# A conformer block's forward and backward pass on one core: b1 placed beside f1, another weight-gradient sum in b6, and the dK/dV partials added by TensorE instead of VectorE

## The chip, the cores and the metric

The kernel runs on one core of one Trainium2 chip. The metric is the time of one execution on the device, in microseconds (us). The names of the engines in the profile are PE (TensorE matmul), PEld (TensorE weight load), DVE (VectorE), ACT (ScalarE), POOL (GpSimd) and SP (SyncE, which issues most DMAs here).

## The reference, cut to what matters

The reference computes a branchformer block and all its gradients, for B = 2, T = 4000, D = 512, in bf16.

```python
def _fwd_reference(x, w_qkv, w_att_out, w_mlp_in, dw_csgu, w_mlp_out, dw_merge, w_merge):
    xa = _layernorm(x)
    q, k, v = split(xa @ w_qkv)
    p = softmax(q @ k.T * D ** -0.5)
    glob = (p @ v) @ w_att_out
    u, g = split(gelu(xa @ w_mlp_in))
    gc = depthwise_conv31(_layernorm(g), dw_csgu)
    loc = (u * gc) @ w_mlp_out
    m = concat(glob, loc)
    m = m + depthwise_conv31(m, dw_merge)
    return x + m @ w_merge

def reference(..., grad_out):
    out, vjp = jax.vjp(_fwd_reference, ...)
    return (out, *vjp(grad_out))      # 9 outputs
```

## The kernel before

The kernel is a sequence of stages, each a Python generator. Some run alone; some run as a main stage with a side stage that `interleave` feeds in between. A scheduler then orders the instructions of each engine at compile time, so an instruction may be placed ahead of its place in the program when its inputs are expected earlier. The order on the chip is fixed.

| stage | what it does |
|---|---|
| f1 | layer norm of x, Q, K, V, the two halves of the MLP, layer norm of g |
| f2 with f3, f4 | softmax attention; beside it the first convolution and `w_mlp_out` |
| f5, f6 | second convolution; output and the gradient of `w_merge` |
| b1 | gradient of m: `grad_out @ w_merge.T`, stored transposed |
| b2 | backward of the second convolution |
| b6 | gradient of the attention output, and of `w_att_out` |
| b7 with b3, b4, b5, weight gradients | attention backward; beside it everything of the local branch |
| b8 | gradients of x and `w_qkv` |

b1 depends on `grad_out` and `w_merge` only, and still stands alone after f6:

```python
    run_gen(gen_f1(k, x, w_qkv, w_mlp_in))
    ...
    run_gen(gen_f6(k, x, w_merge, grad_out, out_0, out_8))
    run_gen(gen_b1(k, grad_out, w_merge))
    # b2 ...
    run_gen(gen_b6(k, w_att_out, out_3))
```

b6 sums its weight gradient over all rows in four PSUM banks that it holds throughout (cut):

```python
        ps = ...tile_pool(name="b6_ps", bufs=2, space=PSUM)
        pst = ...tile_pool(name="b6_pst", bufs=2, space=PSUM)
        acc = psa.tile([128, 4, 512], F32, name="acc")
        ...
                    for dc in range(4):
                        nc.tensor.matmul(acc[:, dc, :], lhsT=attn[...], rhs=dgl[:sz, :], start=(it == 0), stop=(it == ntot - 1))
```

b7 splits the queries of a batch into four parts of eight tiles. For each part it walks over the 32 key tiles; for each key tile it sums dK and dV over the part's queries in two PSUM banks. Between parts the sums are kept in DRAM (`dkvp_d`) in bf16, and from the second part on (`hi > 0`, three quarters of the key tiles, 192 of 256) the stored partial is added on VectorE (cut):

```python
    ps_acc = ...tile_pool(name="b7_psacc", bufs=1, space=PSUM)     # dVacc, dKacc: one bank each
    ps_p   = ...tile_pool(name="b7_psp", bufs=2, space=PSUM)       # pp
    ...
                        for ii, qi in enumerate(half):
                            for c in range(4):
                                nc.tensor.matmul(pp, lhsT=dATh[...], rhs=VTb[...], ...)
                            nc.vector.scalar_tensor_tensor(out=dS, in0=pp, scalar=delta, in1=Eh, ...)   # (pp - delta) * Eh
                            nc.tensor.matmul(dVacc, lhsT=Eh[...], rhs=dAh[...], start=(ii == 0), stop=(ii == nh - 1))
                            nc.tensor.matmul(dKacc, lhsT=dS, rhs=Qh[...], start=(ii == 0), stop=(ii == nh - 1))
                            nc.tensor.transpose(out=pt, in_=dS, identity=k.ident)
                            evac(dSTg[...], pt)                                  # ScalarE
                        ...
                        else:      # hi > 0
                            nc.sync.dma_start(out=part[:ksz, :, :], in_=dst_part)
                            nc.vector.tensor_tensor(out=sumt[:ksz, 0, :], in0=dKacc[:ksz, :], in1=part[:ksz, 0, :], op=ALU.add)
                            nc.vector.tensor_tensor(out=sumt[:ksz, 1, :], in0=dVacc[:ksz, :], in1=part[:ksz, 1, :], op=ALU.add)
                            fin = wk.tile([128, 2, D], BF16, name="fin")
                            nc.scalar.copy(out=fin[:ksz, 0, :], in_=sumt[:ksz, 0, :])       # scaled in the last part
                            nc.scalar.copy(out=fin[:ksz, 1, :], in_=sumt[:ksz, 1, :])
                            nc.sync.dma_start(out=(dst_fin if last else dst_part), in_=fin[:ksz, :, :])
```

## Time and profile before

7046.74 us, median of 4 runs (7039.87 to 7050.35); the profiled run spans 7032.9 us.

The head of the page of the kernel before: span, busy time of each engine, and for 40 equal slices the busy share of TensorE and its granted clock, in tenths.

```profile
span 7032.9 us, 117349 instructions
PE 6004.2 (85%) x46132; PEld 3342.9 (48%) x46132; DVE 4098.4 (58%) x9164; ACT 2932.2 (42%) x6454; POOL 678.1 (10%) x502
PE   6775899799988788787888888899888899999999
PEclk8887999999999999999999999999999999999999
```

TensorE is the busiest engine, but not evenly: the first four slices (0 to 703 us), which hold f1 and its lead-out, are the emptiest and have the lowest clock.

The same kernel, busy times by stretches that I cut at the first and last matmuls of the stages: f1 with its lead-out, f2, f5 and f6, b1 and b2, b6, b7, b8. The columns are the stretch, its length, busy us of PE, PEld, DVE, ACT and POOL with instruction counts, granted clock, DMA share, GB/s.

```profile
0.00:657.80 657.80, 408.82 (x2572) 220.20 (x2573) 358.42 (x1249) 265.44 (x473) 7.22 (x22) 0.82 0.58 190
657.80:2062.30 1404.50, 1285.04 (x8123) 633.33 (x8123) 633.80 (x1715) 619.06 (x1379) 4.90 (x6) 0.97 0.41 101
2062.30:2655.50 593.20, 483.10 (x4806) 311.05 (x4805) 430.60 (x483) 238.91 (x283) 64.00 (x32) 0.95 0.49 166
2655.50:3080.50 425.00, 343.73 (x4050) 251.23 (x4049) 285.17 (x346) 259.21 (x344) 13.68 (x17) 0.95 0.46 161
3080.50:3268.90 188.40, 155.05 (x1048) 80.83 (x1045) 120.13 (x206) 85.51 (x144) 77.90 (x25) 0.95 0.78 249
3268.90:6502.40 3233.50, 2821.30 (x22658) 1601.89 (x22656) 1979.12 (x4489) 1361.02 (x3590) 436.51 (x336) 0.95 0.63 147
6502.40:7032.90 530.50, 507.14 (x2886) 244.42 (x2885) 291.12 (x678) 103.04 (x242) 73.87 (x64) 0.98 0.40 130
```

f1 has TensorE busy for 409 of 658 us; b7 for 2821 of 3233.5 us (87%).

Who TensorE waited for in f1 (30 to 600 us), then who waited for b7's VectorE sums; the columns are total us, times, longest:

```profile
PE pt L469 <- DVE gn L465: 132.2, 16, 8.8
PE pt L405 <- DVE xn L401: 37.6, 16, 30.0
...
PE dVacc L1163 <- DVE sumt L1189: 13.4, 2, 12.1
...
PE dKacc L1164 <- DVE sumt L1188: 1.5, 3, 0.8
```

In f1 TensorE waits for VectorE's two layer norms. The 30.0 us are the start of the kernel, before TensorE's first matmul. In b7 TensorE waited for the sums only 15 us in total.

The transposes of qkT and of gn in f1 of the kernel before (ns: shortest/median/longest), and, from the chain of waits at the end of b8, twelve dense matmuls of 512 columns (start, us, what):

```profile
L423 PE MATMUL pt<-ident,qkT x512: 216/219/230, 42.9 to 575.5; 128*128 128x128 bf16 x165, 128*32 128x128 bf16 x6
L469 PE MATMUL pt<-ident,gn x256: 182/314/314, 65.3 to 595.2; 128*128 128x128 bf16 x124, 32*128 32x32 bf16 x4
...
6970.30 2.62 PE pm L1255 x12
```

The median transpose takes 314 ns here, against 219 ns where TensorE runs densely. The Trainium skill ("TensorE: Matmul & The Clock Gate", Part 1) says why: TensorE's clock falls to half after an idle window of about 3.4 us. The trace agrees. The first transposes of gn come after 8.6 us of idle TensorE, and a few microseconds later TensorE runs densely; the two stretches, with the columns of the table above (the granted clock is the third number from the end):

```profile
65.30:67.30 2.00, 1.89 (x16) 1.62 (x16) 1.89 (x9) 1.04 (x2) 0.00 (x0) 0.50 0.04 14
77.00:80.00 3.00, 2.96 (x37) 2.22 (x36) 1.27 (x3) 2.83 (x6) 0.00 (x0) 1.00 0.47 154
```

At a granted clock of 0.50 the transposes of gn take 314 ns, at 1.00 those of qkT take 219 ns. A dense matmul of 512 columns takes 2.62 / 12 = 0.218 us; the same page, Part 2, gives 215.7 ns start to start at full clock, about 1% less.

Costs of the groups in b7 that the change touches, and of the one at its heart (dS), in the kernel before: busy us and mean ns of one, then the idle time before them and who ended it.

```profile
L1188 DVE TENSOR_TENSOR sumt<-dKacc,part 128x512 f32<-128x512 f32 x192 | 132.2, 688 | 74.1 <-PE dKacc L1164 55.6 <-DMA part<-dkvp_d 16.7 <-PE sA L648 0.5
L1189 DVE TENSOR_TENSOR sumt<-dVacc,part 128x512 f32<-128x512 f32 x192 | 132.1, 688 | 13.6 <-ACT fin L1194 3.8 <-ACT fin L1192 3.2 <-PE dVacc L1163 2.9
L1161 DVE SCALAR_TENSOR_TENSOR dS<-pp,delta_all,Eh 128x128 bf16<-128x128 f32 (+3 forms) x2048 | 654.8, 342 | 500.9 <-PE pp L1159 459.4 <-DMA Eh<-E_d 15.7 <-PE pt L1166 4.0
```

### The profile page before, as it was taken

The page shows a single profiled execution, that of the slowest core. Times are in us where ns is not written, and L with a number is a line of the kernel's source. Part 1 is how long each engine was busy: PE and PEld are TensorE (multiplying, and loading weights), DVE is VectorE, ACT ScalarE, POOL GpSimd, SP SyncE. Part 2 cuts the span into 40 slices and gives each one's busy share as a digit, 9 for nine tenths or more (in the row PEclk, how much of TensorE's full clock was granted, in tenths as well). Part 3 has the DMA queues.
Part 4 walks back from the last instruction along what each step waited for, and adds up shares of the span by engine and source line. Part 5 has one row for each costly group of instructions (what it writes and reads, how often), then busy time and mean ns, then how long its engine had stood idle before and what let it go on. Part 6 is the DMA issues. An engine that isn't in the chain of part 4 may idle for free. (4 is left out here: it accounts for less than half of the span.)

```text
span 7032.9 us, 117349 instructions
## 1 busy us (share of the span) xinstructions
PE 6004.2 (85%) x46132; PEld 3342.9 (48%) x46132; DVE 4098.4 (58%) x9164; ACT 2932.2 (42%) x6454; POOL 678.1 (10%) x502
## 2 busy tenths in 40 slices
PE   6775899799988788787888888899888899999999
PEld 3332444344446444654444455455444555554444
DVE  5663444344449663876777655444898454544555
ACT  3443444344447313764444434333555333333211
POOL 0000000000000110023444100000232000000111
PEclk8887999999999999999999999999999999999999
DMA  5555334535324655466444687877544868763533
GB/s 187 180 194 177 79 89 91 119 76 142 133 81 168 196 162 167 152 211 203 149 135 135 154 127 146 132 163 154 156 135 129 186 142 174 153 155 100 165 119 107
DMA packets 1253003, 1024.07 MB, mean 146 GB/s; under 512 B 486314, under 2 KB 1165057, under 8 KB 1244256
## 3 DMA queue, kind: packets, MB, share of 16 engines
q1 hardware_dynamic: 1214768, 979.15, 52.6%
q10 hardware_dynamic: 37680, 37.43, 1.6%
q8 instruction: 360, 5.90, 0.4%
q14 instruction: 195, 1.60, 0.1%
HBM read 609.16 MB, written 407.25 MB: 145 GB/s over the span
## 5 line engine op out<-in xcount | busy, mean ns | idle before, releaser
L80 ACT COPY dSTg<-pt 128x128 bf16<-128x128 bf16 (+3 forms) x2048 | 538.9, 263 | 1003.1 <-PE pt L1166 909.5
L1161 DVE SCALAR_TENSOR_TENSOR dS<-pp,delta_all,Eh 128x128 bf16<-128x128 f32 (+3 forms) x2048 | 654.8, 342 | 500.9 <-PE pp L1159 459.4
L1159 PE MATMUL pp<-VTb,dATh 128*128 128x128 bf16 (+1 forms) x8192 | 866.3, 222 | 9.0 <-DMA VTb<-VT_d 8.3
L1164 PE MATMUL dKacc<-Qh,dS 128*128 128x512 bf16 (+3 forms) x2048 | 747.5, 395 | 58.8 <-DVE dS L1161 46.0
L1159 PEld LDWEIGHTS <-dATh 128*128 128x128 bf16 (+1 forms) x8192 | 599.2, 100 | 295.2 <-issue 95.6
L1163 PE MATMUL dVacc<-dAh,Eh 128*128 128x512 bf16 (+3 forms) x2048 | 670.1, 387 | 23.8 <-DVE sumt L1189 13.4
L1201 PE MATMUL pq<-Kg,dSTg 128*128 128x512 bf16 (+3 forms) x2048 | 543.9, 384 | 43.1 <-DVE dQacc L1205 34.8
L517 PE MATMUL pm<-KT,QT 128*128 128x512 bf16 (+2 forms) x2048 | 518.1, 378 | 72.0 <-DMA KT<-KT_d 44.5
L548 PE MATMUL po<-V,ET 128*128 128x512 bf16 (+2 forms) x2048 | 507.8, 383 | 3.9 <-DVE ET L82 1.2
L1166 PE MATMUL pt<-ident,dS 128*128 128x128 bf16 (+3 forms) x2048 | 452.5, 221 | 32.9 <-ACT dSTg L80 27.3
L518 DVE TENSOR_SCALAR_CACHE_REDUCE S_sb<-pm 128x512 f32<-128x512 f32 (+2 forms) x512 | 344.2, 675 | 189.6 <-PE pm L517 185.2
L527 ACT ACTIVATE E<-S_sb,nb 128x512 bf16<-128x512 f32 (+2 forms) x512 | 356.9, 699 | 189.0 <-DVE nb L523 189.0
L1164 PEld LDWEIGHTS <-dS 128*128 128x128 bf16 (+3 forms) x2048 | 200.6, 99 | 314.6 <-DVE dS L1161 151.9
L1201 PEld LDWEIGHTS <-dSTg 128*128 128x128 bf16 (+3 forms) x2048 | 193.4, 98 | 262.7 <-issue 99.0
L517 PEld LDWEIGHTS <-QT 128*128 128x128 bf16 (+1 forms) x2048 | 188.8, 98 | 255.6 <-issue 81.3
L548 PEld LDWEIGHTS <-ET 128*128 128x128 bf16 (+2 forms) x2048 | 188.6, 98 | 222.7 <-issue 32.0
L617 POOL MEMSET Xw<- 128x896 bf16 x48 | 39.1, 847 | 2375.4 <-PE sA L648 833.4
L1205 DVE TENSOR_TENSOR dQacc<-dQacc,pq 128x512 f32<-128x512 f32 x192 | 131.3, 684 | 204.4 <-PE pq L1201 204.1
L1166 PEld LDWEIGHTS <-dS 128*128 128x128 bf16 (+3 forms) x2048 | 203.3, 99 | 80.9 <-issue 22.8
L1163 PEld LDWEIGHTS <-Eh 128*128 128x128 bf16 (+3 forms) x2048 | 183.0, 99 | 108.2 <-issue 45.6
L539 PE MATMUL pt<-ident,E 128*128 128x128 bf16 (+2 forms) x2048 | 195.4, 220 | 43.4 <-ACT E L527 40.4
L82 DVE COPY ET<-pt 128x1024 bf16<-128x1024 bf16 (+1 forms) x128 | 86.9, 679 | 236.8 <-PE pt L539 236.8
(278 smaller groups left out, 11117.2 us busy)
## 6 DMA issues: line engine op xcount, KB each, us to landing
E_d<-E SPq DMA_DIRECT2D x62, 1000.0 KB
part<-dkvp_d SPq DMA_DIRECT2D x186, 256.0 KB
Eh<-E_d SPq DMA_DIRECT2D x90, 512.0 KB
Kg<-K_d SPq DMA_DIRECT2D x248, 128.0 KB
dkvp_d<-fin SPq DMA_DIRECT2D x124, 256.0 KB
VTb<-VT_d SPq DMA_DIRECT2D x120, 256.0 KB
XT<-mT_d SPq DMA_DIRECT2D x16, 1536.0 KB
xn<-xn_d SPq DMA_DIRECT2D x42, 512.0 KB
```

The costliest lines, as they stand in the source:

```text
L80: self.nc.scalar.copy(out=out, in_=in_)
L517: nc.tensor.matmul(pm[:sq, :kw], lhsT=QT[:, c, :sq], rhs=KT[:, c, k0:k0 + kw], start=(c == 0), stop=(c == 3))
L518: nc.vector.tensor_scalar(out=S_sb[:sq, k0:k0 + kw], in0=pm[:sq, :kw], scalar1=1.0, scalar2=None, op0=ALU.mult, op1=ALU.max, accum_out=mx[ ...
L527: nc.scalar.activation(out=E[:sq, k0:k0 + kw], in_=S_sb[:sq, k0:k0 + kw], func=ACT.Exp, scale=scale, bias=nb[:sq], accum_out=ls[:sq, kb:kb ...
L539: nc.tensor.transpose(out=pt[:kwj, jj, :sq], in_=E[:sq, kj0:kj0 + kwj], identity=k.ident[:sq, :sq])
L548: nc.tensor.matmul(po[:sq, :], lhsT=ET[:kwj, j, :sq], rhs=V[:kwj, j, :], start=(j == 0), stop=(j == ntile - 1))
L1159: nc.tensor.matmul(pp[:sq, :ksz], lhsT=dATh[:, c, ii * 128:ii * 128 + sq], rhs=VTb[:, c, ks0:ks0 + ksz], start=(c == 0), stop=(c == 3))
L1161: nc.vector.scalar_tensor_tensor(out=dS[:sq, :ksz], in0=pp[:sq, :ksz], scalar=k.delta_all[:sq, col:col + 1], in1=Eh[:sq, ii, ks0:ks0 + ksz ...
L1163: nc.tensor.matmul(dVacc[:ksz, :], lhsT=Eh[:sq, ii, ks0:ks0 + ksz], rhs=dAh[:sq, ii, :], start=(ii == 0), stop=(ii == nh - 1))
L1164: nc.tensor.matmul(dKacc[:ksz, :], lhsT=dS[:sq, :ksz], rhs=Qh[:sq, ii, :], start=(ii == 0), stop=(ii == nh - 1))
L1166: nc.tensor.transpose(out=pt[:ksz, :sq], in_=dS[:sq, :ksz], identity=k.ident[:sq, :sq])
L1201: nc.tensor.matmul(pq[:sq, :], lhsT=dSTg[:ksz, slot, ii, :sq], rhs=Kg[:ksz, slot, :], start=(gi == 0), stop=(gi == len(gsubs) - 1))
```

## The change

The intent is to fill f1's TensorE gaps with b1, to give b6 more PSUM banks in rotation, and to take the two adds per key tile off VectorE: TensorE itself puts the stored partial into the bank, by a matmul with the identity, before the sums begin. The core of the diff (cut; unused new parameters left out):

```diff
-    run_gen(gen_f1(k, x, w_qkv, w_mlp_in))
+    with ExitStack() as region:
+        sps = region.enter_context(tc.tile_pool(name="sps_f1", bufs=1, space=PSUM))
+        main = gen_f1(k, region, x, w_qkv, w_mlp_in)
+        side = gen_b1(k, grad_out, w_merge, sps, ["sA"], sps, "sB", bufs=1, act_every=1)
+        interleave(main, side, B * len(k.tblocks) * 6, b1_units(k), finish_frac=0.9)
...
-    run_gen(gen_b1(k, grad_out, w_merge))
...
-        ps_mm = ctx.enter_context(tc.tile_pool(name="f1_psmm", bufs=4, space=PSUM))
+        ps_mm = ctx.enter_context(tc.tile_pool(name="f1_psmm", bufs=3, space=PSUM))
...  b6: evictions of the transposes all on ScalarE, and
-                        nc.tensor.matmul(acc[:, dc, :], ..., start=(it == 0), stop=(it == ntot - 1))
+                for dc in range(4):
+                    pw = ptile([128, 512], F32)          # 4 banks in rotation, with pm
+                    for j, (s0, sz) in enumerate(subs):
+                        nc.tensor.matmul(pw[:, :], ..., start=(j == 0), stop=(j == len(subs) - 1))
+                    wacc_add(k, first, wacc[:, dc, :], pw[:, :], dc)      # VectorE, into SBUF
...  b7:
+                        have_part = hi > 0
+                        if have_part:
+                            part = wk.tile([128, 2, D], BF16, name="part")
+                            nc.sync.dma_start(out=part[:ksz, :, :], in_=dst_part)
+                            nc.tensor.matmul(dKacc[:ksz, :], lhsT=k.ident[:ksz, :ksz], rhs=part[:ksz, 0, :], start=True, stop=False)
+                            nc.tensor.matmul(dVacc[:ksz, :], lhsT=k.ident[:ksz, :ksz], rhs=part[:ksz, 1, :], start=True, stop=False)
...
-                            nc.vector.tensor_tensor(out=sumt[:ksz, 0, :], in0=dKacc[:ksz, :], in1=part[:ksz, 0, :], op=ALU.add)
-                            nc.vector.tensor_tensor(out=sumt[:ksz, 1, :], in0=dVacc[:ksz, :], in1=part[:ksz, 1, :], op=ALU.add)
-                            ...two ScalarE casts of sumt...
+                            nc.scalar.copy(out=fin[:ksz, 0, :], in_=dKacc[:ksz, :])      # scaled in the last part
+                        nc.vector.tensor_copy(out=fin[:ksz, 1, :], in_=dVacc[:ksz, :])
```

In this text the third piece is called the fold, and its matmuls the seeds.

More of the change, by code (lines that the diff above doesn't have):

```diff
@@ L39, in chain, with delay @@
         yield from g
+def delay(n):
+    for _ in range(n):
+        yield
 def interleave(main, side, main_units, side_units, finish_frac=0.85):
@@ L309 @@
         run_gen(gen_conv(k, k.dm2T_d, k.dmcT_d, k.Zmb_d, C2, "b2", pst, "pt", psc, "po", bufs=2, onchip_out=True))
+    with ExitStack() as region:
+        psp = region.enter_context(tc.tile_pool(name="b6_ps", bufs=2, space=PSUM))
+        pst = region.enter_context(tc.tile_pool(name="b6_pst", bufs=3, space=PSUM))
+        run_gen(gen_b6(k, w_att_out, out_3, psp, ["pm", "pw"], pst, "pt", bufs=2))
     if STOP_AFTER == "b2":
         return debug_dump(k, [k.dmcT_d], keep=(0, 8))
-    run_gen(gen_b6(k, w_att_out, out_3))
     with ExitStack() as region:
@@ L371, in debug_dump, with gen_f1 @@
         zero_range(f0, si * per + cnt, (si + 1) * per if si < len(srcs) - 1 else n0)
-def gen_f1(k, x, w_qkv, w_mlp_in):
+def gen_f1(k, ctx, x, w_qkv, w_mlp_in):
     nc, tc, B, T, D = k.nc, k.tc, k.B, k.T, k.D
-    with ExitStack() as ctx:
+    if True:
         wp = ctx.enter_context(tc.tile_pool(name="f1_w", bufs=1))
@@ L596, in conv_units, with gen_conv @@
     return (C // 128) * per
-def gen_conv(k, src_d, dst_d, Z_d, C, tag, pst, tag_t, psc, tag_c, bufs=1, act_every=2, onchip_out=False):
+def gen_conv(k, src_d, dst_d, Z_d, C, tag, pst, tag_t, psc, tag_c, bufs=1, act_every=2, onchip_out=False, ctx_ext=None, xw_bufs=None, z_bufs=2):
     nc, tc, B, T = k.nc, k.tc, k.B, k.T
@@ L602, in gen_conv @@
     HC = 64
-    with ExitStack() as ctx:
+    with ExitStack() as ctx_own:
+        ctx = ctx_ext if ctx_ext is not None else ctx_own
         gtp = ctx.enter_context(tc.tile_pool(name=tag + "_gt", bufs=bufs))
-        xwp = ctx.enter_context(tc.tile_pool(name=tag + "_xw", bufs=bufs))
+        xwp = ctx.enter_context(tc.tile_pool(name=tag + "_xw", bufs=(xw_bufs or bufs)))
         wtp = ctx.enter_context(tc.tile_pool(name=tag + "_wt", bufs=bufs))
@@ L608, in gen_conv @@
         if onchip_out:
-            zp = ctx.enter_context(tc.tile_pool(name=tag + "_z", bufs=2))
+            zp = ctx.enter_context(tc.tile_pool(name=tag + "_z", bufs=z_bufs))
         evac = Evac(nc, act_every)
@@ L813, in gen_f6, with b1_units, gen_b1 @@
         yield
-def gen_b1(k, grad_out, w_merge):
+def b1_units(k):
+    return k.B * len(k.tblocks) * 3
+def gen_b1(k, grad_out, w_merge, psp, tags, pst_pool, tag_t, bufs=2, act_every=2):
     nc, tc, B, T, D = k.nc, k.tc, k.B, k.T, k.D
@@ L820, in gen_b1, with ptile @@
         wp = ctx.enter_context(tc.tile_pool(name="b1_w", bufs=1))
-        io = ctx.enter_context(tc.tile_pool(name="b1_io", bufs=2))
-        ps = ctx.enter_context(tc.tile_pool(name="b1_ps", bufs=4, space=PSUM))
-        pst = ctx.enter_context(tc.tile_pool(name="b1_pst", bufs=3, space=PSUM))
-        wmgT = load_wT(k, wp, pst, w_merge, "wmgT")
+        io = ctx.enter_context(tc.tile_pool(name="b1_io", bufs=bufs))
+        wmgT = load_wT(k, wp, pst_pool, w_merge, "wmgT", tag=tag_t)
         zero_pads(k, k.dm2T_d, C2)
-        evac = Evac(nc)
+        evac = Evac(nc, act_every)
+        ti = [0]
+        def ptile(shape, dt):
+            ti[0] += 1
+            return psp.tile(shape, dt, name=tags[ti[0] % len(tags)])
         for b in range(B):
@@ L833, in gen_b1 @@
                 for j, (s0, sz) in enumerate(subs):
-                    pt = pst.tile([128, 4, 128], BF16, name="pt")
+                    pt = pst_pool.tile([128, 4, 128], BF16, name=tag_t)
                     for c in range(4):
@@ L837, in gen_b1 @@
                     evac(doT[:, :, s0:s0 + sz], pt[:, :, :sz])
+                yield
                 dm2T = io.tile([128, 8, 512], BF16, name="dm2T")
                 for cc in range(8):
-                    pm = ps.tile([128, 512], F32, name="pm")
+                    pm = ptile([128, 512], F32)
                     for c in range(4):
@@ L843, in gen_b1, with wacc_add @@
                     evac(dm2T[:, cc, :w], pm[:, :w])
+                    if cc == 3:
+                        yield
                 store_dpart(k, nc.sync, k.dm2T_d[0:C2, b, :], 16 + t0, w, dm2T)
                 yield
-def wacc_add(k, first, acc_ap, ps_ap, i):
+def wacc_add(k, first, acc_ap, ps_ap, i, tmp_pool=None):
     nc = k.nc
     if first:
-        if i % 2:
+        if i % 2 or tmp_pool is not None:
             nc.scalar.copy(out=acc_ap, in_=ps_ap)
@@ L854, in wacc_add @@
             nc.vector.tensor_copy(out=acc_ap, in_=ps_ap)
+    elif tmp_pool is not None:
+        t = tmp_pool.tile([128, 512], F32, name="wacc_tmp")
+        nc.scalar.copy(out=t[:], in_=ps_ap)
+        nc.gpsimd.tensor_tensor(out=acc_ap, in0=acc_ap, in1=t[:], op=ALU.add)
     else:
@@ L1023, in gen_b5, with b6_units, gen_b6 @@
         yield
-def gen_b6(k, w_att_out, out_3):
+def b6_units(k):
+    return k.B * len(k.tblocks) * 2 + 1
+def gen_b6(k, w_att_out, out_3, psp, tags, pst_pool, tag_t, bufs=2):
     nc, tc, B, T, D = k.nc, k.tc, k.B, k.T, k.D
@@ L1029, in gen_b6, with ptile @@
         wp = ctx.enter_context(tc.tile_pool(name="b6_w", bufs=1))
-        io = ctx.enter_context(tc.tile_pool(name="b6_io", bufs=2))
+        io = ctx.enter_context(tc.tile_pool(name="b6_io", bufs=bufs))
         wk = ctx.enter_context(tc.tile_pool(name="b6_wk", bufs=2))
-        ps = ctx.enter_context(tc.tile_pool(name="b6_ps", bufs=2, space=PSUM))
-        pst = ctx.enter_context(tc.tile_pool(name="b6_pst", bufs=2, space=PSUM))
-        psa = ctx.enter_context(tc.tile_pool(name="b6_psa", bufs=1, space=PSUM))
-        waoT = load_wT(k, wp, pst, w_att_out, "waoT")
-        acc = psa.tile([128, 4, 512], F32, name="acc")
-        ntot = B * k.ntile
-        it = 0
-        evac = Evac(nc)
+        waoT = load_wT(k, wp, pst_pool, w_att_out, "waoT", tag=tag_t)
+        wacc = wp.tile([128, 4, D], F32, name="wacc_ao")
+        evac = Evac(nc, act_every=1)
+        ti = [0]
+        def ptile(shape, dt):
+            ti[0] += 1
+            return psp.tile(shape, dt, name=tags[ti[0] % len(tags)])
+        first = True
         for b in range(B):
@@ L1043, in gen_b6 @@
                 col0 = b * k.ntile + t0 // 128
-                dm2T = io.tile([128, 4, 512], BF16, name="dm2T")
-                load_dpart(k, nc.sync, dm2T, k.dm2T_d[0:D, b, :], 16 + t0, w)
+                dglT = io.tile([128, 4, 512], BF16, name="dglT")
+                load_dpart(k, nc.sync, dglT, k.dm2T_d[0:D, b, :], 16 + t0, w)
                 dmcT = io.tile([128, 4, 512], BF16, name="dmcT")
-                load_dpart(k, dma_eng(k), dmcT, k.dmcT_d[0:D, b, :], t0, w)
-                dglT = io.tile([128, 4, 512], BF16, name="dglT")
-                nc.gpsimd.tensor_tensor(out=dglT[:, :, :w], in0=dm2T[:, :, :w], in1=dmcT[:, :, :w], op=ALU.add)
+                load_dpart(k, nc.sync, dmcT, k.dmcT_d[0:D, b, :], t0, w)
+                nc.gpsimd.tensor_tensor(out=dglT[:, :, :w], in0=dglT[:, :, :w], in1=dmcT[:, :, :w], op=ALU.add)
                 attn = io.tile([128, 4, D], BF16, name="attn")
@@ L1053, in gen_b6 @@
                 datT = io.tile([128, 4, 512], BF16, name="datT")
+                dgl = io.tile([128, 4, D], BF16, name="dgl")
                 for j, (s0, sz) in enumerate(subs):
                     col = col0 + j
-                    pm = ps.tile([128, 512], F32, name="pm")
+                    pm = ptile([128, 512], F32)
                     for e in range(4):
@@ L1062, in gen_b6 @@
                                                    accum_out=k.delta_all[:sz, col:col + 1])
-                    pt = pst.tile([128, 4, 128], BF16, name="pt")
+                    pt = pst_pool.tile([128, 4, 128], BF16, name=tag_t)
                     for c in range(4):
@@ L1066, in gen_b6 @@
                     evac(datT[:, :, s0:s0 + sz], pt[:, :, :sz])
-                    pt2 = pst.tile([128, 4, 128], BF16, name="pt")
+                    pt2 = pst_pool.tile([128, 4, 128], BF16, name=tag_t)
                     for c in range(4):
                         nc.tensor.transpose(out=pt2[:sz, c, :], in_=dglT[:, c, s0:s0 + sz], identity=k.ident[:])
-                    dgl = wk.tile([128, D], BF16, name="dgl")
-                    evac(dgl[:sz, :], pt2[:sz].rearrange("p c e -> p (c e)"))
-                    for dc in range(4):
-                        nc.tensor.matmul(acc[:, dc, :], lhsT=attn[:sz, j, dc * 128:(dc + 1) * 128], rhs=dgl[:sz, :], start=(it == 0), stop=(it == ntot - 1))
-                    it += 1
+                    evac(dgl[:sz, j, :], pt2[:sz].rearrange("p c e -> p (c e)"))
                 store_tpart(k, nc.sync, k.dattn_d, b, t0, w, dat)
@@ L1077, in gen_b6 @@
                 yield
+                for dc in range(4):
+                    pw = ptile([128, 512], F32)
+                    for j, (s0, sz) in enumerate(subs):
+                        nc.tensor.matmul(pw[:, :], lhsT=attn[:sz, j, dc * 128:(dc + 1) * 128], rhs=dgl[:sz, j, :], start=(j == 0), stop=(j == len(subs) - 1))
+                    wacc_add(k, first, wacc[:, dc, :], pw[:, :], dc)
+                first = False
+                yield
         ot = wk.tile([128, 4, 512], BF16, name="ot3")
-        nc.vector.tensor_copy(out=ot[:], in_=acc[:])
+        nc.vector.tensor_copy(out=ot[:], in_=wacc[:])
         nc.sync.dma_start(out=out_3.rearrange("(c p) e -> p c e", p=128), in_=ot[:])
@@ L1108, in gen_b7 @@
     wk = ctx.enter_context(tc.tile_pool(name="b7_wk", bufs=2))
-    wk1 = ctx.enter_context(tc.tile_pool(name="b7_wk1", bufs=1))
     ps_acc = ctx.enter_context(tc.tile_pool(name="b7_psacc", bufs=1, space=PSUM))
@@ L1153, in gen_b7 @@
                         dKacc = ps_acc.tile([128, D], F32, name="dKacc")
+                        r0 = k0 + ks0
+                        dst_fin = k.dqkv_d[b, r0:r0 + ksz, D:3 * D].rearrange("p (a d) -> p a d", a=2)
+                        dst_part = k.dkvp_d[b, r0:r0 + ksz, :].rearrange("p (a d) -> p a d", a=2)
+                        have_part = hi > 0
[4 more added lines that the diff above has]
+                            nc.tensor.matmul(dVacc[:ksz, :], lhsT=k.ident[:ksz, :ksz], rhs=part[:ksz, 1, :], start=True, stop=False)
                         for ii, qi in enumerate(half):
@@ L1162, in gen_b7 @@
                                                            in1=Eh[:sq, ii, ks0:ks0 + ksz], op0=ALU.subtract, op1=ALU.mult)
-                            nc.tensor.matmul(dVacc[:ksz, :], lhsT=Eh[:sq, ii, ks0:ks0 + ksz], rhs=dAh[:sq, ii, :], start=(ii == 0), stop=(ii == nh - 1))
-                            nc.tensor.matmul(dKacc[:ksz, :], lhsT=dS[:sq, :ksz], rhs=Qh[:sq, ii, :], start=(ii == 0), stop=(ii == nh - 1))
+                            nc.tensor.matmul(dVacc[:ksz, :], lhsT=Eh[:sq, ii, ks0:ks0 + ksz], rhs=dAh[:sq, ii, :], start=(ii == 0 and not have_part), stop=(ii == nh - 1))
+                            nc.tensor.matmul(dKacc[:ksz, :], lhsT=dS[:sq, :ksz], rhs=Qh[:sq, ii, :], start=(ii == 0 and not have_part), stop=(ii == nh - 1))
                             pt = ps_t.tile([128, 128], BF16, name="pt")
@@ L1169, in gen_b7 @@
                                 yield
-                        r0 = k0 + ks0
-                        dst_fin = k.dqkv_d[b, r0:r0 + ksz, D:3 * D].rearrange("p (a d) -> p a d", a=2)
-                        dst_part = k.dkvp_d[b, r0:r0 + ksz, :].rearrange("p (a d) -> p a d", a=2)
-                        if nparts == 1:
-                            fin = wk.tile([128, 2, D], BF16, name="fin")
-                            nc.scalar.activation(out=fin[:ksz, 0, :], in_=dKacc[:ksz, :], func=ACT.Copy, scale=scale)
-                            nc.vector.tensor_copy(out=fin[:ksz, 1, :], in_=dVacc[:ksz, :])
-                            nc.sync.dma_start(out=dst_fin, in_=fin[:ksz, :, :])
-                        elif hi == 0:
-                            part = wk.tile([128, 2, D], BF16, name="part")
-                            nc.scalar.copy(out=part[:ksz, 0, :], in_=dKacc[:ksz, :])
-                            nc.vector.tensor_copy(out=part[:ksz, 1, :], in_=dVacc[:ksz, :])
-                            nc.sync.dma_start(out=dst_part, in_=part[:ksz, :, :])
-                        else:
-                            part = wk.tile([128, 2, D], BF16, name="part")
-                            nc.sync.dma_start(out=part[:ksz, :, :], in_=dst_part)
-                            last = (hi == nparts - 1)
-                            sumt = wk1.tile([128, 2, D], F32, name="sumt")
-                            nc.vector.tensor_tensor(out=sumt[:ksz, 0, :], in0=dKacc[:ksz, :], in1=part[:ksz, 0, :], op=ALU.add)
-                            nc.vector.tensor_tensor(out=sumt[:ksz, 1, :], in0=dVacc[:ksz, :], in1=part[:ksz, 1, :], op=ALU.add)
-                            fin = wk.tile([128, 2, D], BF16, name="fin")
-                            if last:
-                                nc.scalar.activation(out=fin[:ksz, 0, :], in_=sumt[:ksz, 0, :], func=ACT.Copy, scale=scale)
-                            else:
-                                nc.scalar.copy(out=fin[:ksz, 0, :], in_=sumt[:ksz, 0, :])
-                            nc.scalar.copy(out=fin[:ksz, 1, :], in_=sumt[:ksz, 1, :])
-                            nc.sync.dma_start(out=(dst_fin if last else dst_part), in_=fin[:ksz, :, :])
@@ new lines, in gen_b7 @@
+                        last = (hi == nparts - 1)
+                        fin = wk.tile([128, 2, D], BF16, name="fin")
+                        if last:
+                            nc.scalar.activation(out=fin[:ksz, 0, :], in_=dKacc[:ksz, :], func=ACT.Copy, scale=scale)
+                        else:
+                            nc.scalar.copy(out=fin[:ksz, 0, :], in_=dKacc[:ksz, :])
+                        nc.vector.tensor_copy(out=fin[:ksz, 1, :], in_=dVacc[:ksz, :])
+                        nc.sync.dma_start(out=(dst_fin if last else dst_part), in_=fin[:ksz, :, :])
```

## The prediction

> **What bounds the kernel now.** One core, 7032.9 us in the profile, TensorE busy 85% (page). I cut the span by first and last starts of each stage's matmuls and read the busy table by stretches: f1 0-600 us, f2 to f6 up to 2660, b1 2660-2820, b2 to 3080, b6 3080-3275, b7 with its side work 3275-6503, then b8. TensorE is 87% busy in b7 (2818 of 3228 us), 97% where no side work runs (6300-6503). In f1 it is busy only 408 of 570 us; the waits there name VectorE: 132 us for gn, 38 us for xn (layer norm chains). f1's granted clock is 0.84 and its transposes take 314 ns against 219 elsewhere. The Trainium skill ("TensorE: Matmul & The Clock Gate", Part 1) says TensorE falls to half clock after an idle window of about 3.4 us; f1's gn waits of up to 8.8 us agree.
>
> **What changes.**
> 1. b1 moves into f1's gaps. b1 needs 136 us of TensorE and alone takes about 160 us, with about 8 us at each seam. Now it has one PSUM buffer per tag, all evictions on ScalarE (512-wide ones 576 ns), and f1 keeps 3 matmul banks of 4. Load of the joint stage: ScalarE 263 + about 115 = 378 us, TensorE 408 + 136 = 544 us, DMA share about 0.68. At the 88% that TensorE reaches in other interleaved stages it takes about 618 us plus 30 us of start, against 600 + 160: saves about 110 us (60 to 145). One seam fewer: about 10 us more.
> 2. b6: same matmuls. VectorE loses 64 datT copies (413 ns, 26 us), gains 60 adds (683 ns, 41 us); ScalarE gains 37 us; more rotating banks. 195 us becomes about 187.
> 3. b7: for three quarters of the key tiles (192) two 688 ns VectorE adds and about 1.24 us of ScalarE casts become one 679 ns VectorE copy and one ScalarE copy of about 0.6 us: VectorE -134 us, ScalarE -125 us. TensorE gains 384 identity matmuls of 512 columns. Dense chains in b8 run at 0.22 us each (12 in 2.62 us), so +84 us on the engine that bounds b7. What is removed hardly stalled it: matmuls waited for sumt 15 us in total. sumt runs at 3943-5065 and from 5470, mostly where TensorE is 88 to 93% busy and VectorE about 50%; the VectorE-bound stretches (b3 to 3943, most of b5) have none. Some 25 us come back through shorter bank turnover and fewer eviction waits: net +58 us.
>
> **On the critical path:** -110 -10 -8 +58 = -70 us. Predicted 6977 us, 0.99 of before, range 6895 to 7055. Chances: faster by over 2% 0.12, within 2% 0.85, slower 0.03.
>
> **What would show it.** The b1 stretch between f6 and b2 is gone; first softmax matmul at 650 to 700 us (657.8 before); TensorE share in the joint stage 80% or more, clock above 0.84, gn waits well below 132 us. From b7's first matmul to its last pq the span grows by 30 to 85 us, TensorE busy there by about 80, VectorE falls by about 130; waits of the seed matmuls for part under 20 us. b6 180 to 195 us. b8 unchanged.
>
> **What would make it wrong.** If single-buffered b1 units stall TensorE on each ScalarE eviction (about 0.8 us, 9 per block, 16 blocks) the joint stage saves under 50 us. If seeds wait for the part load or for emptied banks at each key tile, b7 loses 150 us or more. If VectorE relief removes more of b7's 410 us of TensorE idle than I think, b7 stays level and the total is near 6920.

## The result, and the profile after

The changed kernel takes 6958.52 us, median of 8 runs (6949.26 to 6975.37), against 7045.73 us for the kernel before in the same rounds (12 runs). The ratio is 0.9878, 95% interval 0.9868 to 0.9888.

The changed kernel by stretches, cut at the same matmuls, with the same columns as before:

```profile
0.00:710.40 710.40, 528.56 (x3373) 273.75 (x3374) 362.76 (x1253) 365.56 (x669) 7.89 (x23) 0.90 0.67 217
710.40:2111.60 1401.20, 1285.54 (x8124) 635.11 (x8124) 634.62 (x1715) 618.97 (x1379) 4.90 (x6) 0.97 0.40 101
2111.60:2707.90 596.30, 485.11 (x4806) 311.74 (x4805) 430.68 (x483) 238.70 (x283) 64.02 (x32) 0.94 0.49 165
2707.90:2977.10 269.20, 207.67 (x3257) 180.11 (x3257) 226.29 (x247) 203.55 (x244) 13.00 (x16) 0.97 0.39 148
2977.10:3152.90 175.80, 153.96 (x1038) 76.52 (x1034) 124.14 (x201) 112.95 (x210) 79.19 (x25) 0.97 0.81 262
3152.90:6432.50 3279.60, 2891.54 (x23045) 1638.56 (x23044) 1885.34 (x4300) 1245.52 (x3398) 436.35 (x336) 0.96 0.63 145
6432.50:6962.70 530.20, 507.43 (x2886) 244.96 (x2885) 291.15 (x678) 103.03 (x242) 73.86 (x64) 0.98 0.40 130
```

Line by line against the table before, in us:

| stretch | before | after | difference |
|---|---|---|---|
| f1 (after: with b1) | 657.8 | 710.4 | +52.6 |
| f2, f5, f6 | 1997.7 | 1997.5 | -0.2 |
| b1 and b2 (after: b2 alone) | 425.0 | 269.2 | -155.8 |
| b6 | 188.4 | 175.8 | -12.6 |
| b7 and its side work | 3233.5 | 3279.6 | +46.1 |
| b8 | 530.5 | 530.2 | -0.3 |
| span | 7032.9 | 6962.7 | -70.2 |

So two pieces gave 116 us and b7 gave 46 us of it back.

TensorE's waits in the joint stage of the changed kernel (30 to 650 us), and the transposes of gn there:

```profile
PE sA L863 <- ACT dm2T L85: 28.5, 44, 1.0
PE pt L480 <- DVE gn L476: 25.1, 9, 8.6
...
PE pt L416 <- DVE xn L412: 5.8, 9, 1.5
...
L480 PE MATMUL pt<-ident,gn x256: 182/229/314, 73.6 to 647.8; 128*128 128x128 bf16 x124, 32*128 32x32 bf16 x4
```

The waits for the layer norms fell from 140 us (without the 30 us at the start) to 31 us, and b1's own work stands in their place. A new wait is small: b1's matmuls wait 28.5 us for ScalarE to empty their single bank. The median transpose fell from 314 to 229 ns and the granted clock of the stretch up to the first softmax matmul rose from 0.82 to 0.90. One gap is left as it was: just before that matmul TensorE is idle for 44 us in both kernels, waiting for the load of KT, and b1 was not placed there.

The groups of b7 in the changed kernel that replace those shown before:

```profile
L1196 PE MATMUL dKacc<-part,ident 128*128 128x512 bf16 x192 | 75.3, 392 | 2.9 <-DMA part<-dkvp_d 0.6 <-ACT fin L1219 0.4
L1197 PE MATMUL dVacc<-part,ident 128*128 128x512 bf16 x192 | 75.3, 392 | 21.8 <-DMA part<-dkvp_d 21.5 <-DVE fin L1220 0.2
L1220 DVE CAST fin<-dVacc 128x512 bf16<-128x512 f32 (+1 forms) x256 | 175.6, 686 | 36.0 <-DMA dkvp_d<-fin 12.2 <-PE sA L717 9.3 <-DMA dqkv_d<-fin 4.4
L1205 DVE SCALAR_TENSOR_TENSOR dS<-pp,delta_all,Eh 128x128 bf16<-128x128 f32 (+3 forms) x2048 | 679.0, 343 | 676.0 <-PE pp L1203 614.6 <-DMA Eh<-E_d 11.4 <-PE dKacc L1208 10.4
```

VectorE now waits for TensorE's pp 615 us before its dS, where it waited 459 us: it became idler. A caution on busy sums: all 2048 dS are in both traces, and 2048 x 342 ns would be 700 us, not 654.8. The busy time is the time that is covered, so instructions that overlap in the trace count once. The stretch table's VectorE difference in b7, -94 us, is the fall of the time in which VectorE is busy at all; the sum of durations fell by more, -264.3 for the sums and +132 for the 192 more dV copies, -132 us.

### The profile page after: what moved, and what is told of

The parts are those of the page before. It is cut to its first block, busy times and chain, and to the rows that moved or that the text cites. A ratio compares the mean times of both kernels' runs of the same rounds, so it can differ in the third digit from the quotient of the medians.

```text
span 6962.7 us, 117900 instructions
## 1 busy us (share of the span) xinstructions
PE 6059.8 (87%) x46516; PEld 3360.7 (48%) x46516; DVE 3955.0 (57%) x8874; ACT 2888.3 (41%) x6424; POOL 679.2 (10%) x502
## 5 line engine op out<-in xcount | busy, mean ns | idle before, releaser
L1205 DVE SCALAR_TENSOR_TENSOR dS<-pp,delta_all,Eh 128x128 bf16<-128x128 f32 (+3 forms) x2048 | 679.0, 343 | 676.0 <-PE pp L1203 614.6
L1203 PE MATMUL pp<-VTb,dATh 128*128 128x128 bf16 (+1 forms) x8192 | 923.6, 221 | 6.7 <-DMA VTb<-VT_d 6.1
L1208 PE MATMUL dKacc<-Qh,dS 128*128 128x512 bf16 (+3 forms) x2048 | 768.9, 393 | 51.3 <-DVE dS L1205 41.6
L1203 PEld LDWEIGHTS <-dATh 128*128 128x128 bf16 (+1 forms) x8192 | 622.2, 99 | 323.7 <-issue 91.9
L1207 PE MATMUL dVacc<-dAh,Eh 128*128 128x512 bf16 (+3 forms) x2048 | 729.1, 386 | 6.8 <-DVE fin L1220 3.4
L1298 POOL TENSOR_TENSOR gx<-t,dot 128x512 bf16<-128x512 f32 x64 | 73.9, 1154 | 1531.0 <-DMA dzT<-dzT_d 1115.6
```

The lines of the kernel that those rows point to most:

```text
L1203: nc.tensor.matmul(pp[:sq, :ksz], lhsT=dATh[:, c, ii * 128:ii * 128 + sq], rhs=VTb[:, c, ks0:ks0 + ksz], start=(c == 0), stop=(c == 3))
L1205: nc.vector.scalar_tensor_tensor(out=dS[:sq, :ksz], in0=pp[:sq, :ksz], scalar=k.delta_all[:sq, col:col + 1], in1=Eh[:sq, ii, ks0:ks0 + ksz ...
L1207: nc.tensor.matmul(dVacc[:ksz, :], lhsT=Eh[:sq, ii, ks0:ks0 + ksz], rhs=dAh[:sq, ii, :], start=(ii == 0 and not have_part), stop=(ii == nh ...
L1208: nc.tensor.matmul(dKacc[:ksz, :], lhsT=dS[:sq, :ksz], rhs=Qh[:sq, ii, :], start=(ii == 0 and not have_part), stop=(ii == nh - 1))
```

## The experiments

The theory, as in the prediction: b1 fills gaps, and the fold is paid by TensorE, which bounds b7, while the VectorE time that it frees was mostly not in the way. Rivals: the fold pays, and b7 is longer for another reason; or the fold's cost is a wait (for the part load, for emptied banks) and not work.

The kernels are built from the changed kernel, or from the kernel before where the label ends in "only". Twelve ran. Each had three or five timed rounds.

### The three pieces one by one

`all_but_fold` is the changed kernel with the b7 of before (the last block of the diff undone); `fold_only`, `b1_only` and `b6_only` are the kernel before with one piece of the diff alone.

> The changed kernel with the old b7 (partials added by VectorE). Theory (TensorE bounds b7, the fold is paid by it): the whole fold is a loss here, b7 goes back from 3280 us to about 3234 us, total about 6913 us, 0.981 of before, clearly faster than the changed kernel. Rival (the fold pays, and the 46 us longer b7 comes from another order of the side work or the new start of the stage): total 6955 us or more.

> The old kernel with the new b7 alone. Theory: b7 grows by 35 to 60 us, total about 7090 us, 1.006 of before; VectorE busy falls by about 100 us or more and buys less than the 70 to 84 us of TensorE work cost. Rival (longer b7 was a side effect of the other two parts): 7045 us or less.

> The old kernel with b1 moved into f1 alone. Theory: saves about 103 us (joint stage +53, stretch after f6 -156), total about 6943 us, 0.985 of before. Rival (part of that gain comes from b6 no longer needing all eight banks behind b2): saves under 90 us.

> The old kernel with the new b6 alone. Theory: 188 us become about 176 us by more rotating banks, total about 7034 us, 0.998 of before, just at the edge of what these rounds resolve. Rival (the b6 gain is due to what runs before it): no difference.

| kernel | median us | ratio to before | 95% interval |
|---|---|---|---|
| all_but_fold | 6913.6 | 0.9827 | 0.9814 to 0.9841 |
| fold_only | 7075.8 | 1.0054 | 1.0040 to 1.0068 |
| b1_only | 6932.5 | 0.9846 | 0.9833 to 0.9860 |
| b6_only | 7027.3 | 0.9982 | 0.9969 to 0.9995 |

Multiplied by 7040 us, b1 gives 108 us, b6 gives 13 us and the fold costs 38 us; the sum, -83 us, is what the changed kernel shows (0.9878, -86 us). Within the noise the pieces simply add up. The rival that the longer b7 came from its neighbours is out: the fold alone lengthens b7 from 3233.5 to 3276.4 us, and without it b7 is back. b7's stretch in `fold_only` and in `all_but_fold`:

```profile
3270.30:6546.70 3276.40, 2898.68 (x23041) 1637.84 (x23039) 1877.80 (x4297) 1246.40 (x3398) 436.40 (x336) 0.95 0.63 145
...
3143.00:6373.80 3230.80, 2819.00 (x22661) 1602.78 (x22660) 1985.58 (x4492) 1360.11 (x3590) 437.21 (x336) 0.95 0.63 147
```

TensorE is 80 us busier with the fold, VectorE 108 us less, ScalarE 114 us less, and the stage is longer by 46 us. `b6_only` shows the b6 stretch falling from 188.4 to 168.5 us in its profile, as much as or more than in the changed kernel, so that gain does not come from what runs before it.

### The fold's cost and its relief, each by itself

`zero_seeds_and_adds` is `all_but_fold` with seeds of zeros and the adds kept:

```diff
+    zseed = res.tile([128, D], BF16, name="zseed");  nc.vector.memset(zseed[:], 0.0)
...
+                        if hi > 0:
+                            nc.tensor.matmul(dKacc[:ksz, :], lhsT=k.ident[:ksz, :ksz], rhs=zseed[:ksz, :], start=True, stop=False)
+                            nc.tensor.matmul(dVacc[:ksz, :], lhsT=k.ident[:ksz, :ksz], rhs=zseed[:ksz, :], start=True, stop=False)
```

> The changed kernel with the old b7 and its VectorE adds, plus 384 identity matmuls of a block of zeros at the places of the seeds: the TensorE cost of the fold by itself, without its relief of VectorE and ScalarE and without waiting for part. Theory (TensorE work is the cost): 55 to 84 us longer than the 6914 us without it, so about 6970 to 6998 us, longer than the changed kernel. Rival (the cost of the fold is the wait for the part load and for the emptied banks at the start of each key tile): under 20 us longer, as zeros are always there.

`no_seeds_no_adds` is the changed kernel without the two seed matmuls (wrong dK and dV; the partials are still loaded and stored, but nothing uses what is loaded):

```diff
-                            nc.tensor.matmul(dKacc[:ksz, :], lhsT=k.ident[:ksz, :ksz], rhs=part[:ksz, 0, :], start=True, stop=False)
-                            nc.tensor.matmul(dVacc[:ksz, :], lhsT=k.ident[:ksz, :ksz], rhs=part[:ksz, 1, :], start=True, stop=False)
```

> The changed kernel with the seed matmuls taken out and nothing in their place; dK and dV are wrong on purpose (they hold the last part of the queries only). The relief by itself. Theory: about 25 to 40 us shorter than the 6914 us with adds (the relief that the prediction put at 25 us), 60 to 84 us shorter than the changed kernel. Rival (VectorE relief is worth nothing here): equal to 6914 us.

`fold_at_end` moves the same two matmuls behind the query loop, as the last of each accumulation (`start=False, stop=True`).

> The changed kernel with the two identity matmuls as the last of each accumulation instead of the first: same TensorE work, same relief, but part is needed some 8 us later. The trace of the changed kernel shows 43 us of weight-load waits for part, 21.5 us of them two stalls of 10.9 us. Theory (work, not waiting): within 20 us of the changed kernel's 6958 us. Rival (waiting for part is most of the cost): 30 us or more faster.

| kernel | adds | seeds | b7 in the profile | median us | ratio, 95% interval |
|---|---|---|---|---|---|
| no_seeds_no_adds | no | no | 3184.0 | 6862.2 | 0.9744 (0.9728 to 0.9759) |
| all_but_fold | VectorE | no | 3230.8 | 6913.6 | 0.9827 (0.9814 to 0.9841) |
| zero_seeds_and_adds | VectorE | zeros | 3270.3 | 6950.0 | 0.9869 (0.9853 to 0.9884) |
| fold_at_end | no | last | 3270.9 | 6951.9 | 0.9872 (0.9858 to 0.9886) |
| changed kernel | no | first | 3279.6 | 6958.5 | 0.9878 (0.9868 to 0.9888) |

b7's stretch in `no_seeds_no_adds`, then `zero_seeds_and_adds`, then `fold_at_end`:

```profile
3148.50:6332.50 3184.00, 2808.88 (x22662) 1595.99 (x22661) 1859.30 (x4300) 1243.37 (x3398) 436.87 (x336) 0.96 0.64 149
...
3150.40:6420.70 3270.30, 2899.20 (x23046) 1638.82 (x23045) 1983.64 (x4493) 1353.53 (x3590) 436.99 (x336) 0.95 0.63 145
...
3150.10:6421.00 3270.90, 2894.40 (x23045) 1634.29 (x23044) 1869.94 (x4300) 1255.82 (x3398) 436.92 (x336) 0.95 0.63 145
```

The first two missed the stated sizes. Zeros cost 40 us of b7 (36 us of the medians), under the 55 to 84 us of the theory and over the 20 us of the rival. Taking both away was worth 47 us of b7 against the adds (25 to 40 expected) and 96 us against the changed kernel (60 to 84 expected). What holds is the structure. With the seeds in, b7 takes 3270 us (3280 in the changed kernel) whether VectorE adds as well or not: against `fold_at_end`, 114 us of VectorE and 98 us of ScalarE work make 0.6 us of difference. Without the seeds, b7 with the adds is 47 us longer than the kernel that leaves them out. And the seeds cost 87 to 96 us on top of that kernel, 40 us on top of the one with adds. The cost of work on two engines here is not a sum. The corner with neither has a wrong result, though, and how much of its 47 us is relief from the adds comes below.

Whether it is work or waiting, `fold_at_end` was meant to tell, and does not: part is needed later there, but its trace still has TensorE waiting 21.0 us for it, in three stalls, where the changed kernel had 21.5 us in two. Its time is not distinguishable from the changed kernel's. The zeros tell it better: they are always there, so their seeds cannot wait for part, and they still lengthen b7 by 40 us. The traces also show that the stalls for part are not new. The two in the changed kernel come 797 and 1094 us after b7's first pp. In the kernel before, TensorE stalls at nearly the same places, 11.0 us at 792 us (for ScalarE's dSTg) and 12.1 us at 1076 us (for VectorE's sum, which was waiting for part).

The cleanest piece is the last part of b7, where no side work is left; its length is read between the last dQ evictions of parts seven and eight. It is 302.8 us without both, 310.6 with the adds and 317.3 in the changed kernel. The seeds' 64 matmuls there account for 14.5 us, which is 0.227 us each, close to the dense rate of 0.218 us. That closeness is not general: the same part takes 312.1 us in `fold_at_end`, so there the same 64 matmuls cost 9.3 us, 0.145 us each.

### Is it VectorE's time, or the emptying of the banks?

`direct_add` adds on VectorE from PSUM straight into the bf16 tile, without the float32 sum and its ScalarE casts. `gpsimd_add` evicts as the changed kernel does, into a float32 tile, and lets GpSimd add; `evict_then_vector_add` is the same with the last add on VectorE.

```diff
+   # direct_add (dK is kept scaled from the first part on)
+   nc.vector.scalar_tensor_tensor(out=fin[:ksz, 0, :], in0=dKacc[:ksz, :], scalar=scale, in1=part[:ksz, 0, :], op0=ALU.mult, op1=ALU.add)
+   nc.vector.tensor_tensor(out=fin[:ksz, 1, :], in0=dVacc[:ksz, :], in1=part[:ksz, 1, :], op=ALU.add)
...
+   # gpsimd_add; nc.vector in place of nc.gpsimd: evict_then_vector_add
+   nc.scalar.activation(out=sumt[:ksz, 0, :], in_=dKacc[:ksz, :], func=ACT.Copy, scale=scale)
+   nc.vector.tensor_copy(out=sumt[:ksz, 1, :], in_=dVacc[:ksz, :])
+   nc.gpsimd.tensor_tensor(out=fin[:ksz, :, :], in0=sumt[:ksz, :, :], in1=part[:ksz, :, :], op=ALU.add)
```

> The changed kernel with b7's partials added by VectorE straight from PSUM into the bf16 output tile (dK kept scaled from the first part on), so the float32 sum and its two ScalarE casts are gone and no TensorE work is added. Same VectorE time as before, ScalarE about 240 us less. Theory (TensorE bounds b7): 0 to 25 us below the 6914 us of the version without the fold, so 6890 to 6914 us and the fastest so far. Rival (VectorE time matters): no gain over 6914 us, or a loss if the scaled add takes longer than 0.69 us.

> The changed kernel with neither seeds nor VectorE adds: dK is evicted by ScalarE (scaled) and dV by VectorE into a float32 tile, as in the run without seeds and adds, and GpSimd, which is idle in these stretches, adds the stored partial. Right result. If the 51 us of relief measured there hold with the add done elsewhere: 6860 to 6885 us, 0.974 to 0.978 of before, over 2% faster and the fastest of all. Rival (GpSimd slows VectorE while both work in SBUF, or its add of about 2.3 us per key tile delays the stores): 6900 us or more.

> The same kernel as the one with the add on GpSimd, but the add from the float32 tile on VectorE. Banks are emptied as early (one copy on each of two engines, side by side), VectorE works more (about 0.68 us of copy and 1.4 to 2.8 us of add per key tile). Theory A (the relief is the earlier emptying of the two banks): b7 near 3184 us, total 6860 to 6890 us. Theory B (the relief is VectorE's time between two dS): b7 as long as with the adds from PSUM or longer, 3230 us or more, total 6910 us or more.

| kernel | b7 in the profile | median us | ratio, 95% interval |
|---|---|---|---|
| direct_add | 3222.5 | 6910.5 | 0.9813 (0.9799 to 0.9827) |
| gpsimd_add | 3223.5 | 6908.4 | 0.9812 (0.9799 to 0.9826) |
| evict_then_vector_add | 3253.0 | 6935.6 | 0.9852 (0.9839 to 0.9866) |

b7's stretch in `gpsimd_add`, then in `evict_then_vector_add`:

```profile
3154.20:6377.70 3223.50, 2825.76 (x22661) 1613.17 (x22660) 1881.84 (x4300) 1246.13 (x3398) 846.35 (x528) 0.95 0.64 148
...
3162.80:6415.80 3253.00, 2849.40 (x22662) 1602.86 (x22661) 2072.04 (x4492) 1250.33 (x3398) 439.13 (x336) 0.95 0.64 146
```

The add of the partial in `gpsimd_add`, then in `evict_then_vector_add`:

```profile
L1219 POOL TENSOR_TENSOR fin<-sumt,part 128x1024 bf16<-128x1024 f32 x192 | 408.3, 2128 | 1606.6 <-ACT sumt L1217 777.8 <-ACT dSTg L85 434.9 <-DVE dS L1196 175.2
...
L1219 DVE TENSOR_TENSOR fin<-sumt,part 128x1024 bf16<-128x1024 f32 x192 | 235.9, 1230 | 64.0 <-ACT sumt L1217 43.0 <-DMA part<-dkvp_d 20.7
```

`evict_then_vector_add` missed the number of its theory A: each bank is emptied by one copy, on two engines, as without the adds, and b7 takes 3253 us, not 3184. Its VectorE is busy 190 us more than in `gpsimd_add` (2072 against 1882) and b7 is 30 us longer. VectorE's time does have a price there, as theory B says. `direct_add` takes 207 us from ScalarE (1360 to 1153 us) and gains 8 us in b7; ScalarE is hardly the limit. Its 6910.5 us cannot be told from the 6913.6 us of `all_but_fold`, so this run does not decide between its theory and its rival.

`gpsimd_add` missed. On TensorE, VectorE and ScalarE it does the work of `no_seeds_no_adds`, yet b7 is 3223.5 us, not 3184. GpSimd did not slow VectorE: its adds took 2128 ns and the mean dS 342 ns, as in `all_but_fold`. So of the 47 us between `all_but_fold` and `no_seeds_no_adds`, only 7 us came back when the adds left VectorE with a right result, although VectorE was about as free (1882 against 1859 us busy) and the banks were emptied in the same way. The 47 us can therefore not be put down to these two alone. Where the other 40 us went is open. They are not spread evenly: cut at the last dQ evictions, the fourth of b7's eight parts takes 392.8 us in `gpsimd_add` and 388.8 in `all_but_fold`, but 367.8 in `no_seeds_no_adds`, which alone is 25 and 21 us. There TensorE is busy 348 us at a granted clock of 0.98, against 356 us at 0.96 in `gpsimd_add`. The two kernels differ in what depends on part, in what the stores wait for, and in the compile-time order of every engine; no run here separates these.

### The joint stage

`b1_evict_alternate` lets VectorE and ScalarE take turns at b1's evictions; `b1_two_banks` gives b1's matmuls two banks and f1's two instead of three.

```diff
-        side = gen_b1(k, grad_out, w_merge, sps, ["sA"], sps, "sB", bufs=1, act_every=1)
+        side = gen_b1(k, grad_out, w_merge, sps, ["sA"], sps, "sB", bufs=1, act_every=2)         # b1_evict_alternate
+        side = gen_b1(k, grad_out, w_merge, sps, ["sA", "sC"], sps, "sB", bufs=1, act_every=1)   # b1_two_banks
-        ps_mm = ctx.enter_context(tc.tile_pool(name="f1_psmm", bufs=3, space=PSUM))
+        ps_mm = ctx.enter_context(tc.tile_pool(name="f1_psmm", bufs=2, space=PSUM))              # b1_two_banks
```

> The changed kernel with b1's evictions alternating between VectorE and ScalarE instead of all on ScalarE. In the joint stage ScalarE is 59% busy, VectorE 57%, and TensorE waits 41 us for ScalarE's emptying of b1's single banks and 31 us for layer norm on VectorE. Theory (VectorE's layer norm chain is what must not be delayed): first softmax matmul the same or up to 15 us later. Rival (ScalarE's queue holds up b1's single banks): 10 to 25 us earlier.

> The changed kernel with two banks for b1's matmuls and two, not three, for f1's. Of the joint stage's waits 33 us are b1's matmuls waiting for their one bank. Theory (f1's 20 matmul groups per block need their banks more than b1's 8): within 10 us of the changed kernel or slower. Rival (the one bank of b1 is what keeps the joint stage at 710 us): 15 to 30 us faster.

Alternating costs: the first softmax matmul comes at 733.9 us, 23.5 us later than in the changed kernel (the theory had 0 to 15), and the total is 6983.7 us, ratio 0.9920 (0.9906 to 0.9933). TensorE's waits in its joint stage show how:

```profile
PE sA L863 <- DVE dm2T L87: 32.8, 27, 3.5
PE pt L480 <- DVE gn L476: 20.2, 6, 8.6
...
PE sA L863 <- ACT dm2T L85: 8.9, 14, 0.7
```

b1's single bank now waits for VectorE, 1.2 us at a time, which runs half of its evictions beside the layer norms; on ScalarE the same wait was 0.65 us at a time (28.5 us, 44 times). The waits for gn did not grow, so the theory's direction was right and its reason was not: the waits that grew are b1's for VectorE, not those for layer norm. Two banks for b1 (717.2 us, total 6969.4 us, ratio 0.9899, 0.9885 to 0.9912) do not help: b1's 28.5 us wait goes, and the wait for gn rises from 25.1 to 38.4 us, that for doT from 8.2 to 19.2.

### The fastest version

Leaving the fold out beats both kernels: 0.9827 for `all_but_fold`, 0.9813 and 0.9812 for the two other ways to add, whose intervals overlap with it. None of the three is shown to be over 2% faster than the kernel before, as each interval reaches past 0.98. Against the kernel before that is about 130 us (0.0188 x 7040), against the changed kernel 36 to 46 us (0.9878 less 0.9827 or 0.9812).

## Why the prediction was right or wrong

The time was right: 6977 us predicted, 6958.5 measured, inside the range, and "within 2%" was the class. The sum of its terms was -70 us; the profiles give -70.2 us, the timed rounds -86 us. That the first two agree to 0.2 us is luck: b1 saved 17 us less than forecast, the fold cost 12 us less and b6 gave 5 us more.

- **b1 (-110 and -10 predicted).** Right, at 12 to 17 us under the sum. The stretches give +52.6 - 155.8 = -103 us, the piece alone 108 us. The way was the foreseen one: waits for the layer norms fell from 140 to 31 us, the joint stage has TensorE busy for 526 us of the 620 between 30 and 650 us (85%), and the clock rose. The feared stall of b1's single banks was there but small, 28.5 us and not 9 x 16 x 0.8 = 115 us, as each wait lasted 0.65 us, and there were 44, not 144.
- **The window for the first softmax matmul (650 to 700 us)** did not follow from the prediction's own numbers: 648 us for the joint stage plus the 58 us that lay between f1's end and that matmul make 706. Measured: 710.4. That was a slip of writing, not of the sum.
- **b6 (-8 predicted, 180 to 195 us).** Right in sign; 175.8 us lies below the stated window. The piece alone gave 13 us.
- **The fold (+84, -25, net +58).** The net was close: +46 in the profile, 38 us (fold_only) in the timed rounds. The mechanism, that TensorE pays for what VectorE saves, is shown by the experiments: seeds of zeros lengthen b7. But the two terms were mis-sized, and nearly cancelled. Put the seeds in first, and they cost 40 us and not 84; take the adds out after that, and not 25 us come back but none (b7 grows by 0.6 to 9 us). Take the adds out first, and 47 us come back in the kernel with a wrong result, 7 us in `gpsimd_add`; the seeds then cost 96 us (87 at the end) or 56 us. The step that failed is "Some 25 us come back", and with it the adding of two fixed terms: what each is worth depends on whether the other is there. I took the 25 us from TensorE's direct waits for sumt (15 us) and a guess. That the net still came out near 58 us is in part luck.
- **Seeds' waits for part under 20 us.** Wrong by little: 21.5 us before the matmuls, in two stalls of 10.9 us at most. TensorE stalled about as long at the same places in the kernel before.
- **TensorE +80, VectorE -130 in b7.** +70 by busy time; -94 by busy time, -132 by the sum of durations.
- **b8 unchanged.** Right.

## What to carry to other kernels

Work that depends on the inputs alone belongs in the gaps of a stage whose busiest engine waits on another one's chain of small operations; here 136 us of TensorE work cost 53 us there, and its evictions did better on the engine that does not run that chain (23.5 us). Before moving an add from VectorE to TensorE, look at which engine bounds that very stretch: here 384 identity matmuls of 0.22 us cost more than the two VectorE adds and the two casts per tile had. And do not add up the gains and costs of engines that share a pipeline: measure the four corners (neither, one, the other, both), as one of the terms may be free once the other is there, and keep the result right in each corner if you can: the corner that broke it here was 40 us faster than one with the same work on three engines and a right result.

## What the Trainium skill lacked or had wrong

- "TensorE: Matmul & The Clock Gate", Part 4, says that the full clock does not engage for transposes and gives about 275 ns for one in a kernel. Here the median transpose took 219 to 221 ns in dense stretches, at a granted clock of 1.00 (77 to 80 us), and 314 ns at 0.50, so transposes among matmuls do run at the full clock. Whether transposes alone would raise the clock, and whether these matmuls with the identity carry the page's transpose mode, no run here shows.
- The same page, Part 2 (Back-to-back issue gap), gives about 131 ns per matmul of 512 columns for a sustained stream with weight loads. Here twelve in a row took 2.62 us, 218 ns each, near the page's other figure of 215.7 ns; the lower one was not seen, as no matmul of 512 columns in the traces before and after is followed by the next in under 214 ns.
- "GPSIMD Engine Reference", section 4.1, calls GpSimd about twice as slow as VectorE for two-input elementwise work. The same 128x1024 add (float32 and bf16 into bf16) took 2128 ns on GpSimd and 1230 ns on VectorE, 1.7 times; and as the GpSimd adds cost no VectorE time there (mean dS 342 ns, as in `all_but_fold`), moving them was still no loss (6908.4 us against 6913.6).
- No page says what identity matmuls cost as a way to load a PSUM accumulator, against an add at eviction. In the part of b7 without side work it was 0.227 us of the stage per 128x512 seed placed first and 0.145 us placed last; with the adds kept, 384 seeds cost b7 40 us, 0.10 us each.
